# Block products for the whole second layer, worked in quarters, with sums from the float32 values

## The chip, the cores and the metric

The kernel runs on one core of one Trainium2 chip. The metric is the device time of one execution in microseconds, of which the median over the runs is given. The core has five engines that run side by side and wait for one another through semaphores: TensorE (matmul; PE in the profile, PEld for its weight loads), VectorE (DVE), ScalarE (ACT), GpSimd (POOL) and SyncE (SP, which here issues DMAs).

## The reference

An attention with window and block summaries over q, k, v of 2 x 8 x 768 x 64 gives a matrix x of 1536 tokens by 512 features. Two feed-forward layers with 2048 hidden features follow. They take most of the time:

```python
def _moe_ref(x, w_in, w_out):
    h = x @ w_in
    relu6 = np.clip(h + 3.0, 0.0, 6.0)
    g = h * relu6 / 6.0
    return g @ w_out

def _moe2_ref(x, w_in, w_out):
    h = x @ w_in
    g = h * (1.0 / (1.0 + np.exp(-h)))
    return g @ w_out
```

## The kernel before

Every float32 factor is split into a high part that TensorE takes in its one-pass float32 type (fp32r) and the low rest, and a product is made of three matmuls: high x high, high x low, low x high. Weights come from memory as float64, two 32-bit words each, and are turned into float32 by VectorE and ScalarE in the steps `conv_mag`, `conv_low`, `conv_clamp`, `conv_join`, `conv_sign`; `conv_hi` (ScalarE or VectorE) then writes the high part and `conv_lo` (GpSimd or VectorE) the low part into a weight slot. A weight group is 128 hidden features: half h = 2n is its columns of w_in, 2n + 1 its rows of w_out. There are 16 groups per layer, 32 in all, n = 0 to 31.

Tokens are worked in three blocks j = 0, 1, 2 of 512. One step (a line of `STEPS`) is one weight group with one token block: `hidden` makes h in a PSUM bank (12 matmuls of 512 columns, in two parts of six), `act` (ScalarE) and `gate` (VectorE) make g, `gate_hi` and `gate_lo` split it, and `project` adds its second product to four accumulators in four PSUM banks (12 matmuls, in two parts of six). `close` does the same for the last two steps, accumulator by accumulator. When all groups of a chunk are through, `finish` takes the accumulators out: the first chunk of a token block is copied to SBUF by ScalarE, a later one is added there by VectorE (`fold` for one in between, `finish` for the last, which also stores it or, in the first layer, makes x of the second: `finish` casts the high part, `finish_lo` makes the low part).

The first layer and the first half of the second (8 groups) go in halves of 8 groups per token block. In the second half of the second layer token block 2 goes first, in the plain way, and blocks 0 and 1 follow in two quarters of four groups. There the first product of two token blocks with two weight groups, a 2 x 2 block product over halves of the features, is made by seven block products instead of eight (Strassen-Winograd): `tsum` (lines 879 to 891) makes four sums of token parts and `ssum` (903 to 919) four sums of weight parts for each pair p of groups, from the high and low parts that lie in the slots; `t_hi`, `t_lo`, `s_hi` and `s_lo` split them; `prod` (931 to 950) is one block product of six matmuls of 512 columns; `keep` and the joins `u2`, `vee`, `u4`, `c22`, `c21`, `c12`, `c11` add the products up on VectorE; the four results go on as steps of `PAIR` through `act`, `gate`, `gate_hi`, `gate_lo` and `project`.

The order of all work is the list `ORDER`, written out in the file (1893 entries before, 1985 after). Each engine takes its operations in the order of that list; an asterisk puts a copy, cast or subtraction on VectorE instead of ScalarE or GpSimd. Buffers are rings that are handed out in the same order: 12 weight slots (`ws`), 3 buffers of words as fetched, 2 of bits, 1 of magnitudes, 3 of gates (`gs`), 8 PSUM banks. `grow` adds buffers when earlier data is gone; in the kernel before, the buffers of the conversion are given to the sums and to the products' results when the last weight is converted. SyncE issues the weight fetches (`fetch`) and the stores.

Of the kernel before, what the change touches and what calls it, by code (L numbers as in the profile page):

```python
# [20 lines left out]
P = 128  # L21
# [9 lines left out]
KD = DM // P  # L31
# [16 lines left out]
def shape_constants():  # L48
# [34 lines left out]

def chunk_of(i):
    layer, half, o, _, f = STEPS[i]
    j = o // WIDE
    if layer == half == 1 and j < 2:
        return layer, half, j, f // QUARTER
    return layer, half, j
# [4 lines left out]
FIRST = {  # L94
# [9 lines left out]
for p in range(HALF // 2):  # L104
    i = next(n for n, s in enumerate(STEPS) if s == (1, 1, 0, WIDE, 2 * p))
    for n, name in ((i, "k"), (i + 1, "v"), (i + QUARTER, "u"), (i + QUARTER + 1, "d")):
        PAIR[n] = (name, p)

# [78 lines left out]
mixed_hi 23, normal 22*, turn 22, turned 22, conv_join 19, conv_mag 20, project 14 0, project 14 1, project 13  # L187
0, project 13 1, fetch 23, mixed_lo 23, conv_clamp 20, conv_low 20, fetch 22, conv_sign 20, conv_join 20,
load_v 22, mix 22, act 15, gate 15, gate_hi 15*, conv_hi 19*, gate_lo 15, project 15 0, project 15 1, conv_hi
20*, conv_lo 20, mixed_hi 22*, mixed_lo 22, grow 3, mixed_hi 20, fetch 21, mixed_lo 20, hidden 17 0, conv_lo  # L190
19*, conv_low 22, conv_low 21, conv_sign 21, hidden 16 0, hidden 16 1, conv_mag 21, conv_clamp 21, conv_join
21, conv_hi 21*, conv_mag 22, conv_clamp 22, conv_sign 22, conv_join 22, conv_hi 22*, conv_lo 22*, conv_lo
21*, grow 4, conv_mag 23, conv_clamp 23, finish 0 0 1 0, conv_low 23, fetch 24, finish 0 0 1 3, conv_sign 23,
conv_join 23, hidden 20 0, finish 0 0 1 2, hidden 17 1, act 17, gate 17, gate_hi 17*, conv_hi 23*, hidden 21
0, hidden 21 1, fetch 30, hidden 20 1, hidden 18 0, act 16, gate 16, gate_hi 16, gate_lo 16, project 16 0,
project 16 1, act 20, gate 20, conv_lo 23, conv_mag 24, conv_clamp 24, conv_low 24, hidden 22 0, conv_sign 24,
conv_join 24, conv_hi 24*, conv_lo 24*, gate_lo 17, act 21, gate 21, hidden 22 1, gate_hi 21*, gate_lo 21,
fetch 26, conv_low 26, hidden 18 1, act 18, gate 18, fetch 25, conv_low 25, gate_hi 20, conv_sign 25, conv_mag
25, project 21 0, project 21 1, hidden 19 0, hidden 19 1, act 22, project 17 0, conv_clamp 25, conv_join 25,
conv_sign 26, gate 22, project 17 1, conv_mag 26, conv_clamp 26, conv_join 26, conv_hi 25, conv_lo 25*,  # L200
gate_hi 22, gate_lo 22, project 22 0, fetch 27, conv_low 27, gate_hi 18*, gate_lo 18, conv_sign 27, conv_hi
26, project 18 0, project 18 1, conv_mag 27, conv_clamp 27, project 22 1, hidden 24 0, conv_join 27, conv_hi
27, conv_lo 27, act 19, gate 19, gate_hi 19, hidden 26 0, conv_lo 26*, hidden 26 1, fetch 28, conv_low 28,
gate_lo 20, project 20 0, conv_mag 28, conv_clamp 28, gate_lo 19, fetch 29, project 19 0, conv_sign 28,
conv_low 29, conv_join 28, conv_hi 28*, act 26, conv_lo 28*, conv_sign 29, conv_mag 29, conv_clamp 29,
conv_join 29, conv_hi 29*, conv_lo 29*, conv_mag 30, conv_clamp 30, hidden 24 1, act 24, conv_low 30,
conv_sign 30, hidden 23 0, hidden 23 1, conv_join 30, gate 26, project 20 1, conv_hi 30, fetch 33, fetch 31,
conv_lo 30*, hidden 29 0, hidden 29 1, conv_mag 31, act 23, gate 23, conv_low 31, conv_sign 31, gate_hi 23,
gate_lo 23, gate_hi 26, gate_lo 26, project 23 0, fetch 35, conv_clamp 31, conv_join 31, conv_hi 31*, conv_lo
31*, fetch 32, conv_mag 32, project 19 1, project 23 1, conv_low 32, conv_clamp 32, conv_sign 32, finish 0 0 2  # L210
3, conv_join 32, conv_hi 32*, gate 24, gate_hi 24*, conv_lo 32, conv_low 33, hidden 30 0, conv_mag 33, hidden
30 1, finish 0 0 2 1, act 30, gate 30, finish 0 0 2 0, fetch 34, hidden 28 0, conv_clamp 33, conv_sign 33,
conv_join 33, conv_low 34, finish 0 0 2 2, act 29, gate 29, hidden 28 1, conv_sign 34, fetch 37, conv_mag 34,
conv_clamp 34, gate_lo 24, act 28, gate 28, hidden 27 0, hidden 27 1, hidden 25 0, gate_hi 29, project 24 0,
gate_lo 29, project 29 0, project 24 1, project 29 1, conv_join 34, conv_hi 33*, conv_lo 33, conv_hi 34*,
conv_lo 34, act 27, gate_hi 28, gate_lo 28, hidden 34 0, hidden 34 1, finish 0 0 1 1, project 26 0, conv_mag
35, conv_clamp 35, conv_low 35, conv_sign 35, conv_join 35, gate_hi 30*, act 34, project 26 1, fetch 36,
conv_low 36, hidden 35 0, conv_hi 35*, gate 27, hidden 31 0, hidden 31 1, conv_mag 36, conv_clamp 36, gate_lo
30, hidden 25 1, conv_sign 36, conv_join 36, gate_hi 27*, gate_lo 27, gate 34, project 27 0, project 27 1, act
31, act 25, gate 25, gate_hi 25, conv_lo 35, conv_low 37, project 30 0, project 30 1, fetch 38, hidden 32 0,  # L220
hidden 32 1, gate_lo 25, project 25 0, gate 31, project 25 1, act 32, gate_hi 31, gate_lo 31, project 28 0,
project 31 0, hidden 36 0, finish 0 1 0 1, finish 0 1 0 0, gate 32, gate_hi 32, hidden 37 0, conv_hi 36,
hidden 37 1, hidden 33 0, project 28 1, project 31 1, conv_sign 37, gate_lo 32, project 32 0, finish 0 1 0 3,
finish 0 1 0 2, act 37, conv_mag 37, conv_clamp 37, gate 37, gate_hi 37*, gate_lo 37, conv_lo 36*, hidden 35
1, act 35, hidden 33 1, hidden 39 0, act 33, gate 33, gate_hi 33*, gate_lo 33, fetch 41, project 32 1, project
37 0, project 37 1, conv_low 38, conv_join 37, conv_hi 37*, conv_lo 37*, conv_mag 38, conv_sign 38, hidden 36
1, act 36, gate 36, finish_lo 0 2, hidden 39 1, hidden 40 0, hidden 40 1, gate_hi 36, gate_lo 36, fetch 39,
conv_low 39, project 33 0, project 33 1, act 39, gate 35, gate 39, gate_hi 39*, gate_lo 39, project 36 0,
project 36 1, gate_hi 35*, gate_lo 35, conv_clamp 38, conv_join 38, hidden 38 0, hidden 38 1, project 35 0,
project 35 1, conv_mag 39, hidden 43 0, hidden 43 1, conv_sign 39, conv_clamp 39, conv_join 39, gate_hi 34*,  # L230
gate_lo 34, project 34 0, finish_lo 0 1, project 34 1, conv_hi 38*, conv_lo 38*, act 38, gate 38, fetch 40,
conv_low 40, conv_hi 39, gate_hi 38*, gate_lo 38, conv_mag 40, conv_clamp 40, project 38 0, act 40, act 43,
gate 43, gate 40, project 39 0, gate_hi 40, project 38 1, conv_sign 40, conv_join 40, project 39 1, gate_lo
40, project 40 0, finish 0 1 1 0, conv_lo 39, fetch 45, gate_hi 43, project 40 1, finish_lo 0 0, hidden 41 0,
# [127 lines left out]
def attention_moe_kernel(  # L362
# [765 lines left out]
```

## Time and profile before

| | |
|---|---|
| median of 3 runs | 608.94 us (608.93 to 609.13) |
| the profiled execution | 609.09 us |
| its span, first to last instruction | 607.3 us |
| mean granted TensorE clock | 0.994 |
| TensorE busy | 597.3 us, 3188 matmuls |
| VectorE busy | 459.9 us, 1019 instructions |
| ScalarE busy | 252.3 us |
| GpSimd busy | 70.4 us |

The profile gives one execution. Busy time is the sum of an engine's instructions, overlaps counted once. The chain of waits goes back from the last instruction to what released it at each step. The table by stage gives busy time and instruction counts between two moments.

### The profile page before, as it was taken

The page shows a single profiled execution, that of the slowest core. Times are in us where ns is not written, and L with a number is a line of the kernel's source. Part 1 is how long each engine was busy: PE and PEld are TensorE (multiplying, and loading weights), DVE is VectorE, ACT ScalarE, POOL GpSimd, SP SyncE. Part 2 cuts the span into 40 slices and gives each one's busy share as a digit, 9 for nine tenths or more (in the row PEclk, how much of TensorE's full clock was granted, in tenths as well). Part 3 has the DMA queues.
Part 4 walks back from the last instruction along what each step waited for, and adds up shares of the span by engine and source line. Part 5 has one row for each costly group of instructions (what it writes and reads, how often), then busy time and mean ns, then how long its engine had stood idle before and what let it go on. Part 6 is the DMA issues. An engine that isn't in the chain of part 4 may idle for free.

```text
span 607.3 us, 8702 instructions
## 1 busy us (share of the span) xinstructions
PE 597.3 (98%) x3188; PEld 495.2 (82%) x3188; DVE 459.9 (76%) x1019; ACT 252.3 (42%) x591; POOL 70.4 (12%) x86
## 2 busy tenths in 40 slices
PE   7899999999999999999999999999999999999997
PEld 7778888888888888888888888888888888888786
DVE  4889999586698887537789899624247998888984
ACT  4988877664334344123234453131123333231220
POOL 3483430200000001000001010000001000000000
PEclk9799999999999999999999999999999999999999
DMA  9999965130332342202133333300003000000003
GB/s 250 234 226 258 221 166 122 58 108 15 94 110 98 110 130 76 68 1 69 36 104 105 104 105 114 96 0 1 0 1 104 2 0 1 0 37 17 18 17 122
DMA packets 69051, 51.56 MB, mean 85 GB/s; under 512 B 36368, under 2 KB 63504, under 8 KB 69008
## 3 DMA queue, kind: packets, MB, share of 16 engines
q1 hardware_dynamic: 69008, 51.01, 30.8%
q8 instruction: 25, 0.41, 0.3%
q14 instruction: 18, 0.15, 0.1%
HBM read 47.85 MB, written 3.15 MB: 84 GB/s over the span
## 4 chain that ended last, share of the span: by engine, by line
PE 96%; ACT 2%; DVE 1%; POOL 1%; issue 0%; ACTq 0%
PE bank L721 36%; PE bank L792 22%; PE bank L795 22%; PE bank L950 6%; PE bank L613 3%; PE bank L682 2%; PE bank L670 2%; PE bank L508 1%; PE bank L1046 1%; ACT early_w L642 1%; DVE kmax L522 0%; PE bank L557 0%; PE bank L576 0%; POOL early_units L662 0%; ACT early_w L541 0%
## 5 line engine op out<-in xcount | busy, mean ns | idle before, releaser
L721 PE MATMUL bank<-x,w 128*128 128x512 f32 x768 | 184.9, 391 | 0.0
L721 PEld LDWEIGHTS bank<-x,w 128*128 128x128 f32 x768 | 143.1, 188 | 30.0 <-DVE r L762 0.5
L792 PE MATMUL bank<-g,w 128*128 128x512 f32 x576 | 138.3, 392 | 0.0
L795 PE MATMUL bank<-w,g 128*128 128x512 f32 (+1 forms) x588 | 137.1, 385 | 0.0
L795 PEld LDWEIGHTS bank<-w,g 128*128 128x128 f32 x588 | 108.6, 188 | 23.1 <-DVE g L772 1.0
L792 PEld LDWEIGHTS bank<-g,w 128*128 128x128 f32 x576 | 107.1, 188 | 22.2
L458 POOL TENSOR_TENSOR w<-bits,w 128x512 fp32r<-128x512 f32 x25 | 34.0, 1363 | 349.1 <-ACT w L454 193.5
L772 DVE TENSOR_TENSOR g<-r,g 128x512 fp32r<-128x512 f32 x81 | 55.3, 688 | 24.3 <-ACT g L766 22.1
L418 ACT ACTIVATE mag<-words 128x512 f32<-128x512 f32 x64 | 43.1, 674 | 45.5 <-DVE bits L436 37.2
L750 ACT ACTIVATE r<-bank 128x512 f32<-128x512 f32 x48 | 28.5, 597 | 57.8 <-PE bank L721 49.0
L762 DVE TENSOR_TENSOR r<-bank,r 128x512 f32<-128x512 f32 x28 | 19.1, 687 | 37.6 <-ACT r L752 37.5
L436 DVE SCALAR_TENSOR_TENSOR bits<-mag,bits 128x512 uint32<-128x512 uint32 x64 | 44.3, 693 | 1.6
L721 PE MATMUL bank<-x_late,w 128*128 128x512 f32 x192 | 45.0, 389 | 0.0
L443 DVE SCALAR_TENSOR_TENSOR bits<-words,bits 128x512 uint32<-128x512 uint32 x64 | 44.2, 690 | 1.0
L758 DVE SCALAR_TENSOR_TENSOR r<-r,bank 128x512 f32<-128x512 f32 x48 | 32.5, 682 | 13.9 <-ACT r L750 13.6
L721 PEld LDWEIGHTS bank<-x_late,w 128*128 128x128 f32 x192 | 36.0, 188 | 7.5
L766 ACT CAST g<-r 128x512 fp32r<-128x512 f32 x43 | 26.4, 619 | 30.8 <-PE bank L792 13.7
L752 ACT ACTIVATE r<-bank 128x512 f32<-128x512 f32 x28 | 16.5, 596 | 48.8 <-PE bank L721 46.7
L430 DVE TENSOR_SCALAR mag<-mag 128x512 f32<-128x512 f32 x64 | 30.1, 471 | 4.6 <-ACT mag L418 4.3
L423 DVE TENSOR_SCALAR bits<-words 128x512 uint32<-128x512 uint32 x64 | 28.4, 447 | 1.1 <-DMA words<-in_moe_w_in_dram 0.6
L642 ACT ACTIVATE early_w<-early_w,stat 128x120 f32<-128x120 f32 x72 | 27.5, 385 | 3.8 <-DVE stat L628 3.6
L454 ACT CAST w<-bits 128x512 fp32r<-128x512 f32 x32 | 19.7, 617 | 20.7 <-DVE bits L436 20.7
(160 smaller groups left out, 645.6 us busy)
## 6 DMA issues: line engine op xcount, KB each, us to landing
words<-in_moe_w_in_dram SPq DMA_DIRECT2D x32, 512.0 KB, 3.9
words<-in_moe_w_out_dram SPq DMA_DIRECT2D x32, 512.0 KB, 3.4
early_r<-in_v_dram SPq DMA_DIRECT2D x15, 192.0 KB, 4.4
out_dram<-acc SPq DMA_DIRECT2D x11, 256.0 KB, 2.0
early_w<-in_q_dram SPq DMA_DIRECT2D x10, 256.0 KB, 5.9
stage<-in_k_dram SPq DMA_DIRECT2D x3, 512.0 KB, 5.3
stage<-in_v_dram SPq DMA_DIRECT2D x3, 512.0 KB, 7.3
early_w<-in_v_dram SPq DMA_DIRECT2D x3, 512.0 KB, 5.3
```

The lines of the kernel that those rows point to most:

```text
L418: nc.scalar.activation(out=out, in_=low_high(h)[:, 1].bitcast(F32), func=AF.Abs, scale=EXP_SHIFT)
L430: nc.vector.tensor_scalar(out=mag, in0=mag, scalar1=MAG_MIN, scalar2=MAG_MAX, op0=ALU.max, op1=ALU.min)
L436: nc.vector.scalar_tensor_tensor(out=bits, in0=mags.use(h).bitcast(U32), scalar=3, in1=bits, op0=ALU.logical_shift_left, op1=ALU.bitwise_or,)
L443: nc.vector.scalar_tensor_tensor(out=bits, in0=low_high(h)[:, 1], scalar=0x80000000, in1=bits, op0=ALU.bitwise_and, op1=ALU.bitwise_or,)
L458: eng.tensor_tensor(out=w_half(h, 1), in0=bitss.use(h).bitcast(F32), in1=w_half(h, 0).bitcast(F32), op=ALU.subtract,)
L642: nc.scalar.activation(out=pr[:, hp], in_=pr[:, hp], func=AF.Exp, scale=-1.0, bias=st[:, 0, hp : hp + 1], accum_out=st[:, 1, hp : hp + 1],)
L721: nc.tensor.matmul(ps[:, :n], w[:, a, kk * P : (kk + 1) * P], x[:, o // SUB : (o + n) // SUB, b, kk, :], start=(m == 0), stop=(m == last),)
L758: nc.vector.scalar_tensor_tensor(out=r, in0=r, scalar=6.0, in1=ps, op0=ALU.min, op1=ALU.mult)
L772: eng.tensor_tensor(out=g[:, 1, cols], in0=r[:, cols], in1=g[:, 0, cols].bitcast(F32), op=ALU.subtract)
L792: nc.tensor.matmul(ps[:, o : o + n], lhs, g[:, b, shift : shift + n], **flags)
L795: nc.tensor.matmul(ps[:, : len(cols)], g[:, a, rows], rhs, **flags)
L950: nc.tensor.matmul(ps, lhs, rhs, start=(i == 0), stop=(i == 5))
```

## The change

The whole second layer goes in quarters of four weight groups, each with token blocks 2, 0, 1 in this order, and all eight pairs of its groups use the seven block products for blocks 0 and 1. The accumulators of a quarter are copied out after the first quarter and added after the second and third (`fold`, 24 for 8) and the last. The first layer's second half takes its token blocks in the order 2, 0, 1 too.

The sums are made from the float32 values: `ssum` reads the converted bits before they are split (so these buffers are held longer, `bit_users`, and a third one is laid over the constants once these are done with, `grow 8`), and `tsum` reads the first layer's result in its accumulator buffer; each is one instruction where it was two or three. So the features 0 to 255 of x in token block 1 need no split of their own (`only_in_sums`), and their room holds the split weight sums. The sums and the products' results now need room while weights are still converted: one buffer of words becomes the weight sums (`grow 5`) and one weight slot the token sums (`grow 6`), then results (`grow 7`). The result of a gate in `PAIR` stays in its own buffer and the activation takes a temporary one.

`ORDER` is written anew from the attention's end on (entry 724); before that it is the same. In the new list there are 128 `hidden` for 160, 56 `prod` for 28, 28 more joins, 32 `ssum` for 16, `s_hi` 32 for 16 (11 of them on VectorE, for 8), 32 `s_lo` for 16, 8 `keep` for 4 (two on VectorE), 10 `finish_lo` for 12; of `conv_hi` 25 on VectorE for 32, of `conv_lo` 28 for 39, of `gate_hi` 39 for 43, of `t_hi` one for none.

```diff
+QUARTER = HALF // 2
+BLOCKS = (2, 0, 1)
+STEPS += [(0, 1, j * WIDE, WIDE, f) for j in BLOCKS for f in range(HALF)]
 STEPS += [
-    (layer, half, j * WIDE, WIDE, f)
-    for layer, half in ((0, 1), (1, 0))
-    for j in range(NWIDE)
-    for f in range(HALF)
-]
-
-STEPS += [(1, 1, (NWIDE - 1) * WIDE, WIDE, f) for f in range(HALF)]
-QUARTER = HALF // 2
-STEPS += [
-    (1, 1, j * WIDE, WIDE, q * QUARTER + f)
+    (1, half, j * WIDE, WIDE, q * QUARTER + f)
+    for half in range(2)
     for q in range(2)
-    for j in range(2)
+    for j in BLOCKS
     for f in range(QUARTER)
 ]
...
+for i, s in enumerate(STEPS):
+    if s[0] and s[2] == 0 and s[4] % 2 == 0:
+        for n, name in ((0, "k"), (1, "v"), (QUARTER, "u"), (QUARTER + 1, "d")):
+            PAIR[i + n] = (name, weight_of(i) // 2)
+PAIRED = sorted({p for _, p in PAIR.values()})
...
+    def bit_users(h):
+        n, i = divmod(h, 2)
+        return 2 if i or n // 2 not in PAIRED else 5 - n % 2
...
     def act(i):
-        ps = hidden_of(i, "see")
-        r, cols = room(rs, i, 3)
-        if STEPS[i][0] == 0:
-            nc.scalar.activation(out=r[:, cols], in_=ps[:, : STEPS[i][3]], func=AF.Relu, bias=3.0)
+        kind = dict(func=AF.Sigmoid) if STEPS[i][0] else dict(func=AF.Relu, bias=3.0)
+        if i in PAIR:
+            r, ps = rs.take(("temp", i), 1), rs.see(PAIR[i])
         else:
-            nc.scalar.activation(out=r[:, cols], in_=ps, func=AF.Sigmoid)
+            (r, cols), ps = room(rs, i, 2), banks.use(("h", i))[:, : STEPS[i][3]]
+            r = r[:, cols]
+        nc.scalar.activation(out=r, in_=ps, **kind)
...
+    def fold(n, j, m):
+        ps, part, _, _ = gathered((1, n // 2, j, n % 2), m)
+        nc.vector.tensor_tensor(out=part, in0=ps, in1=part, op=ALU.add)
+
+    def only_in_sums(j, m):
+        return j == 1 and m < KD // 2
...
+            if only_in_sums(j, m):
+                return
+            nc.scalar.copy(out=second_x(j)[:, :, 0, m], in_=halves(part))
...
     def tsum(a):
 
-        out = by_feature(whole_t.take(a, 3 if a < 3 else 2))
-        q = {(k, j, b): quarter(k, j, b) for k in range(2) for j in range(2) for b in range(2)}
+        out = whole_t.take(a, 3 if a < 3 else 2)
         if a % 2 == 0:
-            k, j = (1, 1) if a == 2 else (1, 0)
-            terms = [(q[k, j, 0], None), (by_feature(whole_t.use(a // 2)), ALU.subtract)]
-            add_up(out, terms + [(q[k, j, 1], ALU.add)])
+            x, y = whole_x(1 if a == 2 else 0, 1), whole_t.use(a // 2)
         else:
-            plus, minus = {1: ((0, 1), (0, 0)), 3: ((1, 1), (0, 1))}[a]
-            terms = [(q[*plus, 0], None), (q[*minus, 0], ALU.subtract)]
-            add_up(out, terms + [(q[*plus, 1], ALU.add), (q[*minus, 1], ALU.subtract)])
+            x, y = (whole_x(1, 0), whole_x(0, 0)) if a == 1 else (whole_x(1, 1), whole_x(1, 0))
+        nc.vector.tensor_tensor(out=out, in0=x, in1=y, op=ALU.subtract)
...
-        if k in (1, 3):
-            x, y, op = (a21, a22, ALU.add) if k == 1 else (a11, a21, ALU.subtract)
-            terms = [(x[0], None), (y[0], op), (x[1], ALU.add), (y[1], op)]
+
+        def a(row, col):
+            return bitss.use(2 * (2 * p + row)).bitcast(F32)[:, col * SUB : (col + 1) * SUB]
+
+        if k == 1:
+            x, y, op = bitss.see(4 * p + 2).bitcast(F32)[:, :SUB], a(1, 1), ALU.add
         elif k == 2:
-            terms = [(s[:, 0], None)] + [(x, ALU.subtract) for x in a11]
+            x, y, op = s[:, 0], a(0, 0), ALU.subtract
+        elif k == 3:
+            x, y, op = a(0, 0), a(1, 0), ALU.subtract
         else:
-            terms = [(a12[0], None), (s[:, 1], ALU.subtract), (a12[1], ALU.add)]
-        add_up(s[:, k - 1], terms)
+            x, y, op = a(0, 1), s[:, 1], ALU.subtract
+        nc.vector.tensor_tensor(out=s[:, k - 1], in0=x, in1=y, op=op)
...
         elif n == 5:
...
+            t = words.take("gone", 1)
+            whole_s.free.append(t.bitcast(F32).rearrange("p (k n) -> p k n", k=4))
         elif n == 6:
+            i = slot_number[id(ws.take("gone", 1))]
+            values.append(main.tile([P, 2, 2 * DM], F32, tag=f"w{i}", name="sums"))
+            whole_t.free += [values[0][:, b] for b in range(2)]
+        elif n == 7:
             assert not whole_t.held
-            rs.free += [t[:, o : o + DM] for t in whole_t.free for o in (0, DM)]
+            rs.free += [values[0][:, b, o : o + DM] for b in range(2) for o in (0, DM)]
+        elif n == 8:
+            bitss.free.append(cst[:, :DM].bitcast(U32))
```

## Rows read from the trace of the kernel before

**Rows 1.** The page, busy time, share of the span and instructions of each engine.
```profile
PE 597.3 (98%) x3188; PEld 495.2 (82%) x3188; DVE 459.9 (76%) x1019; ACT 252.3 (42%) x591; POOL 70.4 (12%) x86
```
**Rows 2.** Stages: us, busy us (instructions) per engine, granted clock, DMA share, GB/s.
```profile
core 0: us, PE busy (x) PEld busy (x) DVE busy (x) ACT busy (x) POOL busy (x), PEclk, DMA share, GB/s
...
173.00:339.00 166.00, 166.00 (x734) 137.41 (x733) 126.98 (x228) 57.98 (x100) 12.05 (x9) 1.00 0.27 83
339.00:445.00 106.00, 105.97 (x468) 87.42 (x467) 61.89 (x110) 30.30 (x51) 3.95 (x3) 1.00 0.18 55
445.00:604.20 159.20, 159.11 (x710) 131.09 (x709) 131.55 (x233) 46.93 (x82) 3.88 (x3) 1.00 0.08 27
```
**Rows 3.** The chain that ended last: start us, us, engine, line, instructions.
```profile
445.44 5.44 PE bank L721 x24
...
476.76 1.36 PE bank L950 x6
...
584.91 19.24 PE bank L795 x96
```
**Rows 4.** Waits of TensorE's weight loads, 173 to 604 us: total us, times, longest.
```profile
PEld bank L795 <- DVE g L772: 1.0, 3, 0.4
PEld bank L721 <- DVE r L762: 0.5, 1, 0.5
PEld bank L795 <- DVE g L766: 0.2, 1, 0.2
```
**Rows 5.** Instructions by line and form: busy us, mean ns, idle before them.
```profile
L830 DVE TENSOR_TENSOR acc<-bank,acc 128x512 f32<-128x512 f32 x8 | 5.3, 684 | 2.1 <-PE bank L795 2.1
L959 DVE TENSOR_TENSOR r<-bank,r 128x512 f32<-128x512 f32 x5 | 3.4, 683 | 0.0
L927 DVE TENSOR_TENSOR x<-words,x 128x256 fp32r<-128x256 f32 x16 | 6.5, 418 | 0.1
L923 ACT CAST x<-words 128x256 fp32r<-128x256 f32 x8 | 3.1, 402 | 8.1 <-DVE words L877 8.1
L877 DVE TENSOR_TENSOR words<-words,w 128x256 f32<-128x256 f32 x28 | 11.9, 425 | 0.9
L877 DVE TENSOR_TENSOR words<-words,x 128x1024 f32<-128x1024 f32 x6 | 7.4, 1225 | 0.2
L454 ACT CAST w<-bits 128x512 fp32r<-128x512 f32 x32 | 19.7, 617 | 20.7 <-DVE bits L436 20.7
L454 DVE CAST w<-bits 128x512 fp32r<-128x512 f32 x32 | 13.5, 424 | 0.8
L458 DVE TENSOR_TENSOR w<-bits,w 128x512 fp32r<-128x512 f32 x39 | 26.6, 688 | 0.9
L458 POOL TENSOR_TENSOR w<-bits,w 128x512 fp32r<-128x512 f32 x25 | 34.0, 1363 | 349.1 <-ACT w L454 193.5 <-DVE w L454 135.0 <-PE bank L792 20.5
```
**Rows 6.** VectorE in order of time: start us, duration us, line, operation.
```profile
475.00 0.41 DVE L423 TENSOR_SCALAR bits<-words 128x512 uint32<-128x512 uint32 x1
475.33 0.42 DVE L430 TENSOR_SCALAR mag<-mag 128x512 f32<-128x512 f32 x1
475.67 0.68 DVE L443 SCALAR_TENSOR_TENSOR bits<-words,bits 128x512 uint32<-128x512 uint32 x1
476.38 0.69 DVE L436 SCALAR_TENSOR_TENSOR bits<-mag,bits 128x512 uint32<-128x512 uint32 x1
...
577.13 0.68 DVE L762 TENSOR_TENSOR r<-words,r 128x512 f32<-128x512 f32 x1
577.73 0.68 DVE L959 TENSOR_TENSOR bits<-bank,bits 128x512 f32<-128x512 f32 x1
```
**Rows 7.** Stages of VectorE's dense stretch, columns as in rows 2.
```profile
469.60:491.40 21.80, 21.80 (x98) 18.06 (x97) 21.10 (x34) 8.16 (x14) 0.33 (x1) 1.00 0.03 13
491.40:513.20 21.80, 21.80 (x98) 18.06 (x97) 18.33 (x31) 9.09 (x16) 0.00 (x0) 1.00 0.00 1
513.20:534.90 21.70, 21.70 (x98) 17.96 (x97) 18.68 (x34) 4.46 (x8) 0.00 (x0) 1.00 0.03 13
534.90:556.70 21.80, 21.77 (x96) 17.71 (x95) 18.71 (x38) 6.40 (x12) 0.00 (x0) 1.00 0.06 24
556.70:578.40 21.70, 21.70 (x95) 17.49 (x94) 19.21 (x40) 4.49 (x8) 0.00 (x0) 1.00 0.04 14
```

More of the change, by code (lines that the diff above doesn't have):

```diff
@@ L286 @@
-gate_lo 71, conv_mag 63, conv_clamp 63, prod 1 1, keep 1, gate_lo 72, project 69 0, project 71 0, prod 0 1,
-conv_low 63, conv_sign 63, conv_join 63, finish 1 0 2 0, conv_hi 62*, conv_lo 62*, conv_hi 63, conv_lo 63*,
-grow 5, finish 1 0 2 1, hidden 76 0, project 69 1, hidden 73 0, hidden 73 1, tsum 3, hidden 74 1, hidden 76 1,
-hidden 75 0, tsum 1, hidden 75 1, project 71 1, t_hi 3, ssum 0 1, ssum 0 2, s_hi 0 2*, ssum 0 4, finish 1 0 1
-1, act 73, gate 73, s_hi 0 1*, s_lo 0 1, gate_hi 73, act 75, gate 75, gate_hi 75*, finish 1 0 2 3, t_lo 3,
@@ new lines @@
+ssum 9 3, hidden 48 1, gate 44, gate_hi 44*, gate_lo 44, project 44 0, project 44 1, fetch 40, conv_low 40,
+conv_clamp 39, conv_join 39, conv_hi 39, gate_lo 42, gate 47, act 48, gate_hi 47, gate_lo 47, conv_lo 39, gate
+48, gate_hi 48, conv_mag 40, conv_clamp 40, gate_lo 48, project 42 0, project 47 0, finish 0 1 1 1, fetch 41,
+finish 0 1 1 0, tsum 1, project 42 1, project 47 1, finish 0 1 1 2, conv_low 41, prod 8 1, t_hi 1*, finish 0 1
+1 3, hidden 49 0, t_lo 1, keep 8, finish_lo 1 2, tsum 2, tsum 4, t_hi 2, t_lo 2, t_hi 4, t_lo 4, hidden 49 1,
@@ new lines @@
+project 48 0, tsum 3, prod 9 2, hidden 50 0, ssum 9 2, ssum 9 4, prod 8 2, t_hi 3, conv_sign 40, hidden 51 0,
+hidden 51 1, act 49, gate 49, gate_hi 49, prod 8 6, conv_join 40, conv_hi 40, gate_lo 49, t_lo 3, finish_lo 1
+3, conv_lo 40*, hidden 50 1, act 50, gate 50, gate_hi 50, grow 7, project 49 0, act 51, prod 8 7, conv_mag 41,
+u2 8, vee 8, gate 51, conv_clamp 41, prod 8 3, conv_sign 41, c11 8, act 52, conv_join 41, conv_hi 41, gate 52,
+prod 8 5, u4 8, gate_lo 50, s_hi 9 2, s_lo 9 2, project 48 1, prod 8 4, c22 8, c21 8, project 49 1, gate_hi
@@ new lines @@
+1, ssum 12 2, gate_hi 64*, conv_hi 49*, conv_lo 49, project 62 1, project 63 0, ssum 12 3, fold 1 2 0, project
+63 1, prod 11 6, gate 65, fold 1 2 2, prod 11 7, keep 11, gate_hi 65, conv_hi 50, u2 11, fetch 52, ssum 12 4,
+fetch 51, conv_lo 50*, gate_lo 64, prod 11 5, gate_lo 65, prod 11 3, conv_low 52, vee 11, c22 11, u4 11,
+conv_sign 52, act 71, gate 71, prod 11 4, prod 11 2, project 64 0, conv_low 51, c11 11, conv_sign 51, conv_mag
+51, conv_clamp 51, conv_join 51, s_hi 12 2, s_hi 12 4, s_lo 12 4, c21 11, fetch 53, fold 1 2 3, s_hi 12 3*,
@@ new lines @@
+81*, project 73 0, project 73 1, conv_sign 57, conv_join 57, act 77, gate_hi 74, gate_lo 74, prod 13 6, s_hi
+13 4, conv_mag 58, conv_sign 58, gate_hi 75, project 74 0, project 74 1, gate 77, gate_lo 75, conv_hi 57*,
+s_lo 13 4, conv_lo 57*, project 75 0, fold 2 2 0, project 75 1, conv_clamp 58, act 76, gate 76, gate_hi 76,
+fold 2 2 3, prod 13 1, prod 13 7, s_hi 13 1*, gate_lo 76, conv_lo 56, keep 13, u2 13, fold 2 2 1, c11 13,
+gate_lo 81, hidden 84 0, hidden 84 1, s_lo 13 1, prod 13 5, conv_join 58, ssum 14 1, ssum 14 2, prod 13 3, act
@@ new lines @@
+conv_low 60, prod 14 4, fold 2 0 3, gate_hi 83*, prod 14 1, conv_sign 60, fold 2 0 1, conv_mag 60, conv_clamp
+60, project 80 0, project 81 0, gate 82, fold 2 0 2, ssum 14 4, s_hi 14 4, conv_join 60, conv_hi 60, project
+80 1, s_hi 14 3*, s_lo 14 3, project 81 1, gate_hi 82, hidden 85 0, keep 14*, gate_lo 82, project 82 0,
+project 82 1, conv_mag 61, conv_clamp 61, conv_low 61, conv_sign 61, conv_join 61, gate_lo 83, project 83 0,
+fetch 62, conv_mag 62, conv_clamp 62, project 83 1, fold 2 1 1, fetch 63, fold 2 0 0, conv_lo 60, conv_hi 61,
```

334 lines of the change are left out of this document (155 added, 179 removed).

## The prediction

> **What bounds the kernel now.** I read the page first, then the stages, then the chain of waits, then TensorE's own waits, and last VectorE in its dense stretch. The page puts TensorE at 98% of the span and VectorE at 76% [rows 1]. A busy TensorE need not be at its peak, so the next view decides: from 173 us on TensorE is never out of work. From 339 to 445 us it ran 468 matmuls in 106.0 us, 0.2265 us each, at granted clock 1.00, its higher level [rows 2]. The chain says the same per group: 24 matmuls of 512 columns take 5.44 us and a Strassen-type block product of six takes 1.36 us, so 0.2267 us each whatever the line, and the last 96 before the end stand in one piece [rows 3]. All that its weight loads waited for between 173 and 604 us is 1.0 + 0.5 + 0.2 = 1.7 us, each time for VectorE's gate parts [rows 4]. So a matmul taken away is worth 0.2267 us, as long as VectorE, which feeds it, keeps up.
>
> **The part that gains.** In the second layer the first product of token blocks 0 and 1 with two weight groups takes 2 x 2 x 12 = 48 matmuls in the plain way and 7 x 6 = 42 by block products. The kernel has this for the four pairs of the second half; the change has it for all eight. In the order list 32 `hidden` halves of six go and 28 `prod` of six come: 24 matmuls less, 24 x 0.2267 = 5.44 us. `project` and `close` stay as many, and the quarters change only their order.
>
> **What VectorE and the others get.** Durations of single instructions are not what they cost one behind the other. A 128x512 operation with two inputs is 0.68 to 0.69 us long [rows 5], but the next one starts 0.60 us after it (577.13 to 577.73); one with a single input starts its successor after 0.33 us (475.00, 475.33). Only when the successor reads what was just written is it 0.71 us (475.67 to 476.38) [rows 6]. The shorter ones shrink in proportion, 0.42 to 0.34 us for 256 columns (an estimate from the 0.42 and 0.33 of row 475.00), 1.22 to 1.13 for 1024 (the same 0.09 off). At these steps:
> More: 16 `fold` (24 for 8), as the first half's quarters are added too: 9.6 us. Seven joins for each of four pairs, 28: 16.8. 16 `s_lo`: 5.4. Three more `s_hi`, two `keep` and a `t_hi` here: about 2.6. Together 34.4.
> Less: `ssum` from 40 instructions of 256 columns to 32, mostly dependent ones at 0.45: 3.6. `tsum` from ten of 1024 columns to four: 7.3. 11 `conv_lo` that go to GpSimd: 6.6. Seven `conv_hi` and four `gate_hi` that go to ScalarE: 3.7. Two `finish_lo` dropped: 1.2. Together 22.4.
> Net VectorE +12 us, 460 to some 472 of 604: 78%. By full durations it is +15.
> ScalarE gets 13 `s_hi` at 0.40, seven `conv_hi`, four `gate_hi`, two `keep` and loses two casts and one `t_hi`: about +11 on 252 us. GpSimd gets 11 x 1.36 = 15 on 70 [rows 5]. Neither is near its limit. DMA: the same 64 weight fetches and 13 stores on SP's queue; they are spread over the whole second layer, since one word buffer and one weight slot are given up earlier. I cost them at nothing: what hides them is the slack of the buffers, and if that is gone a fetch, four conversion steps and two casts stand in a row ahead of a `hidden`. The tightest slot reuse that I find in the new list (weight group 27) still has five groups of six matmuls, 6.8 us, over the two steps that must wait for the slot, 0.62 on ScalarE and 1.36 on GpSimd. `s_hi` now waits for nothing of token block 1's first features, as these are only needed in sums; what waits at the layer's start is the chain `tsum`, `t_hi`, `t_lo`, with nine groups (12.2 us) between the first layer's last `project` and the first product that needs it; VectorE's work ahead of that is nine instructions, some 8 us by the same steps.
>
> **Where the load is dense.** More than the total, the share per pair matters. In the new steady state a pair of weight groups costs TensorE 7 products, 2 plain firsts of two halves and 6 seconds of two halves: 23 x 1.36 = 31.3 us. VectorE's share of it, when all four weight parts are converted in that time: 33 two-input instructions (7 joins, 6 gates, 6 `gate_lo`, 4.5 folds and finishes, 8 in conversions, 1.75 `conv_lo`) x 0.60 = 20.0; 12 one-input ones x 0.34 = 4.1; 8 of 256 columns and 1.4 casts, 3.1. That is 27.2 us; some 20 of the steps are dependent and add 0.11 each: 29.4, or 94%. By full durations it is 32.2, or 103%. The row nearest to it is the kernel's own product stretch: from 491.4 to 578.4 us VectorE was busy 18.33 + 18.68 + 18.71 + 19.21 = 74.9 of 87.0 us (86%), and in the 21.8 us before that 21.10 (97%), and TensorE waited for next to nothing [rows 4, 7]. So a short load of 97% is known to be harmless and 86% for long; 94% over several pairs lies between. Only about 24 of the 32 second-layer weight parts are converted that late, so six pairs or so are heavy and the rest lighter. I take 29.4, since the steps of rows 6 were taken in just such a stretch.
>
> Here a page speaks against the change. The steps of rows 6 are shorter than the durations. The Trainium skill, "VectorE: DVE Perf Modes", section "The DRAIN you can't avoid", has it that the next operation cannot issue until the pipeline of the last one has emptied; by it the sum of full durations would count, and the gain would be used up. The trace does not agree for independent operations (0.60 after 0.68).
>
> **The sum.** 608.94 - 5.44 = 603.5. For the places where a gate part comes late I add 0.2, as in the trace's 1.7 us over 431 us they are few: 603.7 us. The profiled execution was 609.09 with a span of 607.3, 0.15 above the median and 1.8 outside the span; I keep both offsets, so the span should be about 602.1. The unknown part is what a fuller VectorE costs TensorE: at best nothing, and half of the 1.7 us of late gates goes too, 603.5 - 0.8 = 602.7; at worst the cases below.
>
> **Rivals.**
> VectorE nearly full. It is busy 94%, and its order is fixed, so a join that waits for its product holds back the gates behind it. Of 4.3 us that it would idle per pair at the 14% of rows 7, only 1.9 are free (31.3 - 29.4); if it keeps 2.3 to 2.6, TensorE loses 0.4 to 0.7 in each of six heavy pairs, 2.4 to 4.2 in all: about 606. For it: the 97% stretch is only 21.8 us long. Against: no wait above 0.5 us in a stretch of 86%.
> Full lengths. If each VectorE step costs its full duration under this mix, a heavy pair is 0.9 us over, six of them 5.4: the gain is just given back, 609. This is what the page's rule would do. Against it: rows 6.
> VectorE becomes the bound (slower). Work 29.4 and waits for products, three quarters of the present 4.3 kept, give 32.6 per heavy pair, 1.3 over TensorE's 31.3; six pairs lose 7.8, less 5.4: 611.3. It decides from 32.2 per pair on (31.3 + 5.44 / 6), that is when 2.8 us of waits cannot be given up. For it: 24 folds instead of 8 must free PSUM banks on the engine that is late. Against: a waiting VectorE has other work listed, and in the product stretch of now its waits cost TensorE nothing.
> The change does not do what it says: the products come but something else of six matmuls stays. The list of operations speaks against it (192 matmuls go, 168 come); time as before.
>
> **Chances.** Forecast 0.62; nearly full 0.18; full lengths or no effect 0.09; VectorE as bound 0.11. Differences under 0.2%, 1.2 us, can't be told from none. So faster 0.80, same 0.09, slower 0.11. The range 602.7 to 608.0 leaves out the last two cases, 0.20.
>
> **What would show it.** Right: 3164 matmuls for 3188; the span near 602; the chain one piece of TensorE from 173 us to the end; weight loads' waits still about 2 us; VectorE about 470 us, never above 97% of a stretch. Wrong: waits of weight loads on gate parts, joins or weight conversions of 3 us and more (nearly full), VectorE at 98% or more over 60 us with TensorE idle beside it (VectorE as bound), or steps of 0.69 us between independent operations (full lengths). A lower granted clock in the second layer would make all of this wrong, as it would show that TensorE idled.

## The result and the profile after

The changed kernel takes 602.77 us in the median (602.37 to 602.98, 4 runs) for 609.04 (608.93 to 609.30) of the kernel before beside it: ratio 0.9896, 95% interval 0.9878 to 0.9913. The gain is 6.27 us; 603.7 was forecast, with a range of 602.7 to 608.0. The profiled execution took 602.95 us with a span of 601.1. In the experiments below one run of one kernel (1452.86 us, *Shorter products*) lies far off the others and is left out of its median.

The page of the changed kernel, its first part:

```profile
PE 590.1 (98%) x3164; PEld 489.4 (81%) x3164; DVE 476.4 (79%) x1047; ACT 261.3 (43%) x614; POOL 86.1 (14%) x97
```

24 matmuls are gone [rows 1] and VectorE is busy for 16.5 us more. The stages of the changed kernel, columns as in [rows 2]:

```profile
0.00:47.89 47.89, 41.24 (x436) 36.09 (x437) 38.37 (x157) 36.15 (x122) 28.87 (x44) 0.96 1.09 244
47.89:172.35 124.46, 123.67 (x848) 101.71 (x847) 102.74 (x294) 80.74 (x238) 20.83 (x27) 1.00 0.49 124
172.35:597.98 425.63, 425.21 (x1884) 351.58 (x1883) 334.90 (x597) 144.44 (x256) 36.41 (x26) 1.00 0.18 56
```

And the kernel before, cut at the same three places of the work (first `hidden`, the attention's end, last matmul):

```profile
0.00:49.55 49.55, 42.73 (x436) 37.57 (x437) 37.87 (x157) 36.56 (x122) 29.56 (x44) 0.93 1.05 238
49.55:173.04 123.49, 123.49 (x848) 101.79 (x847) 101.27 (x294) 80.51 (x237) 20.96 (x27) 1.00 0.49 124
173.04:604.15 431.11, 431.04 (x1909) 355.89 (x1907) 320.36 (x569) 135.21 (x233) 19.87 (x15) 1.00 0.18 55
```

The third line of each is the one that the change touches: 431.11 - 425.63 = 5.48 us, which is 24 x 0.2267 = 5.44 within what such a cut can tell (a matmul record or two are missing). The other 0.69 us of the profiled pair comes from before the first changed operation, where the instructions are the same: 1.66 us less in the first stage and 0.97 more in the second. In the first stage the mean granted clock is 0.93 in the kernel before and 0.96 in the changed one, since TensorE ran at its lower level (half clock) for 6.8 us in the one and for 3.4 us in the other.

The weight loads' waits after 172 us, to be held against [rows 4]:

```profile
PEld bank L809 <- DVE g L786: 1.3, 2, 0.7
```

So TensorE hardly waits. VectorE, though, is dense for much longer than before. The same 200 us of the second layer, first in the kernel before, then in the changed one, which has block products all through it:

```profile
345.00:545.00 200.00, 199.94 (x881) 164.81 (x880) 140.70 (x245) 63.05 (x110) 7.83 (x6) 1.00 0.12 37
345.00:545.00 200.00, 199.58 (x879) 164.57 (x878) 180.05 (x325) 75.45 (x136) 21.06 (x15) 1.00 0.19 58
```

180.05 of 200 us is 90%. The chain that ended last shows it too. Its shares of the span by engine, before and after, and the changed kernel's fullest stage:

```profile
PE 96%; ACT 2%; DVE 1%; POOL 1%; issue 0%; ACTq 0%
PE 86%; DVE 7%; ACT 4%; DMA 1%; issue 1%; SPq 0%; DVEq 0%; ACTq 0%
447.90:469.60 21.70, 21.42 (x95) 17.37 (x93) 21.27 (x38) 10.15 (x19) 3.03 (x2) 1.00 0.23 72
```

From 436 to 470 us the changed kernel's chain runs over VectorE, which is busy 98% (21.27 of 21.70 us) in the middle of it, and the two late gates stand at its end (468.3 and 470.1 us). By time and waits alone one would say that a tenth of VectorE is still free. The experiments say what that tenth is worth.

### The profile page after: what moved, and what is told of

The parts are those of the page before. It is cut to its first block, busy times and chain, and to the rows that moved or that the text cites. A ratio compares the mean times of both kernels' runs of the same rounds, so it can differ in the third digit from the quotient of the medians.

```text
span 601.1 us, 8713 instructions
## 1 busy us (share of the span) xinstructions
PE 590.1 (98%) x3164; PEld 489.4 (81%) x3164; DVE 476.4 (79%) x1047; ACT 261.3 (43%) x614; POOL 86.1 (14%) x97
## 4 chain that ended last, share of the span: by engine, by line
PE 86%; DVE 7%; ACT 4%; DMA 1%; issue 1%; SPq 0%; DVEq 0%; ACTq 0%
PE bank L730 27%; PE bank L806 22%; PE bank L809 19%; PE bank L966 11%; PE bank L622 2%; PE bank L691 2%; PE bank L679 1%; PE bank L517 1%; DMA early_w<-in_k_dram 1%; DVE g L786 1%; PE bank L1063 1%; ACT early_units L651 1%; ACT early_w L651 1%; DVE kmax L531 1%; DVE early_w L637 1%
## 5 line engine op out<-in xcount | busy, mean ns | idle before, releaser
L730 PE MATMUL bank<-x,w 128*128 128x512 f32 x576 | 139.8, 392 | 0.0
L730 PEld LDWEIGHTS bank<-x,w 128*128 128x128 f32 x576 | 107.2, 188 | 22.0 <-DVE x L714 0.2
L786 DVE TENSOR_TENSOR g<-r,g 128x512 fp32r<-128x512 f32 x72 | 52.9, 739 | 16.9 <-ACT g L780 15.5
L759 ACT ACTIVATE r<-bank 128x512 f32<-128x512 f32 x60 | 35.4, 596 | 67.2 <-PE bank L730 50.6
L966 PE MATMUL bank<-w,x 128*128 128x512 f32 x144 | 35.7, 389 | 0.0
L452 DVE SCALAR_TENSOR_TENSOR bits<-words,bits 128x512 uint32<-128x512 uint32 x48 | 34.8, 725 | 0.7
L445 DVE SCALAR_TENSOR_TENSOR bits<-mag,bits 128x512 uint32<-128x512 uint32 x48 | 33.1, 689 | 1.0
L966 PEld LDWEIGHTS bank<-w,x 128*128 128x128 f32 x144 | 27.0, 188 | 5.6
L467 POOL TENSOR_TENSOR w<-cst,w 128x512 fp32r<-128x512 f32 x10 | 14.3, 1425 | 88.2 <-ACT w L463 44.0
L432 DVE TENSOR_SCALAR bits<-words 128x512 uint32<-128x512 uint32 x48 | 22.0, 460 | 3.5 <-DMA words<-in_moe_w_in_dram 1.8
```

The costliest lines, as they stand in the source:

```text
L445: nc.vector.scalar_tensor_tensor(out=bits, in0=mags.use(h).bitcast(U32), scalar=3, in1=bits, op0=ALU.logical_shift_left, op1=ALU.bitwise_or,)
L452: nc.vector.scalar_tensor_tensor(out=bits, in0=low_high(h)[:, 1], scalar=0x80000000, in1=bits, op0=ALU.bitwise_and, op1=ALU.bitwise_or,)
L467: eng.tensor_tensor(out=w_half(h, 1), in0=bitss.use(h).bitcast(F32), in1=w_half(h, 0).bitcast(F32), op=ALU.subtract,)
L730: nc.tensor.matmul(ps[:, :n], w[:, a, kk * P : (kk + 1) * P], x[:, o // SUB : (o + n) // SUB, b, kk, :], start=(m == 0), stop=(m == last),)
L759: nc.scalar.activation(out=r, in_=ps, **kind)
L786: eng.tensor_tensor(out=g[:, 1, cols], in0=r[:, cols], in1=g[:, 0, cols].bitcast(F32), op=ALU.subtract)
```

## The experiments

Times of runs beside different runs of the kernel before are compared by their ratios; the changed kernel's is 0.9896, and 0.990 when it was run again. Where a text speaks of the traced stretch, it is the time in the run's trace from the first matmul behind the attention to the end of the last matmul: 431.26 us before, 425.80 in the changed kernel. The start of a run has no part in it.

**The changed kernel again**, for the start.

> The changed kernel itself, unchanged, beside more runs of the kernel before on one chip. Theory 1 (the change is worth 24 matmuls, 5.4 us; the rest of the 6.2 us came from runs of before that all had 6.8 us of half clock at the start): runs of the two kernels with the same mean granted clock differ by 4.9 to 5.6 us, and the medians by 4.9 to 6.5, as the starts fall. Theory 2 (the change shortens the start too): by 6.0 to 6.5 also at the same granted clock.

Median 603.00 us for 608.98 of before (17 runs): ratio 0.990 (0.988 to 0.992). By granted clock the runs fall into groups. Where the mean clock of the run was 0.996 to 1.0, before took 607.25 to 607.79 and this kernel 602.15 and 601.71: 5.1 to 6.1 apart. Where it was 0.993 or 0.994, before took 608.31 to 610.41 with a median of 609.3 (12 runs), and this kernel 603.00 to 603.67: some 6.2. Theory 1's 5.4 lies inside the first of these only, Theory 2's 6.0 to 6.5 holds the second and touches the first, so the times lean to Theory 2. The traces decide against it. The traced stretch of this run is 425.80 us once more, 5.46 less than before: that is what the change is worth. The moment at which the stretch begins differs between traces of the very same instructions: from 172.18 to 172.88 us in the seven traces with 6.8 us at half clock (before has the latest, `b_less24`, which does the same work up to there, the earliest) and from 171.13 to 172.19 in the five with 3.4 or none. The 0.69 us lie within that. A lower clock at the start costs more than that: between the medians of the two groups of runs, 1.7 us for the kernel before and 1.1 for this one, so two kernels' medians of four runs can differ by as much through it alone. In the first comparison before had 0.994 in its profiled run and this kernel 0.994 to 0.997.

**24 matmuls back.**

```diff
+        again = mms if k == 1 and p < 12 else []
-        for i, (kk, (a, b)) in enumerate(mms):
+        for i, (kk, (a, b)) in enumerate(again + mms):
+            i %= 6
```

> The changed kernel, with 24 matmuls added back: the six matmuls of the first block product of pairs 8 to 11 are issued twice, the second time from the start again, so the result is the same. VectorE's work stays. Theory 1: 602.8 + 5.4 = 608.2. Theory 2 (VectorE sets the pace in the dense stretch): some of the added TensorE time fits into its waits, 603 to 606.5.

607.63 us (607.25 to 609.86, 12 runs), ratio 0.9994 (0.9982 to 1.0006). That is 0.0098 x 609 = 6.0 us above the changed kernel; between runs at a clock of 0.997, 607.5 against 602.15 of the run again (one run, on another chip, on which the kernel before takes the same 607.4 at that clock), 5.4; in the traced stretch, 431.16 for 425.80, 5.36. None of the added time fits into a wait. TensorE paces the changed kernel; Theory 2's 603 to 606.5 falls.

**24 matmuls less, in the kernel before.**

```diff
+        if (layer, half, j) == (1, 0, 0) and f % 2 == 0:
+            if part:
+                return
+            last = cut - 1
```

> The kernel before, with 24 matmuls left out: in the first half of the second layer the second six matmuls of the first product of token block 0 with weight groups 16, 18, 20 and 22 are not issued, so these four hold only two of four feature parts. VectorE's work is as before. Theory 1 (TensorE is the bound, each matmul is worth 0.2267 us, and the changed kernel hides all of VectorE's additional work): 608.9 - 5.4 = 603.5, and 24 matmuls explain 5.4 us of the 6.2 us that the change gained; the other 0.7 us lies in the first 50 us of the run and comes from how long TensorE ran at half clock there, so it shows here only if this run's start does. Theory 2 (VectorE's additional work costs the changed kernel something): this kernel, without that work, is the faster one of the two, below 602.4.

604.74 us (604.03 to 605.91, 6 runs) for 608.51: ratio 0.9945 (0.9928 to 0.9963), a gain of 3.3 to 3.8 and not of 5.4; in the traced stretch, 427.93 for 431.26, it is 3.33. This is slower than either theory had it (603.5, or below 602.4). The waits of its weight loads after 173 us:

```profile
PEld bank L799 <- DVE g L776: 2.6, 5, 1.1
PEld bank L799 <- DVE g L770: 0.8, 2, 0.5
PEld bank L725 <- DVE r L766: 0.6, 1, 0.6
PEld bank L799 <- ACT g L770: 0.4, 1, 0.4
```

4.4 us, for 1.7 [rows 4]. The 2.7 us more stand between 344 and 389 us, in and behind the stretch where the matmuls were left out, and most of them cost time (5.44 - 3.33 = 2.1). TensorE waits there for gate parts, which sit in VectorE's list where the removed matmuls used to give them time. Neither theory had this: here a removed matmul is worth 0.2267 us only if the order is laid out anew, as the change does.

**Both sums at their old length.**

```diff
+            for _ in range(2 if k % 2 == 0 else 3):
+                nc.vector.tensor_tensor(out=s[:, k - 1], in0=x, in1=y, op=op)
```

and the same for `tsum`.

> The changed kernel with the token and weight sums at the instruction counts of the kernel before (ten per pair of weight groups, ten for the tokens), by issuing the one instruction two or three times; the values are the same. VectorE gets 48 instructions of 256 columns at 0.34 and 6 of 1024 at 1.13: 16.3 + 6.8 = 23 us. Theory 1 in its strong form (VectorE has room for it): 602.8. Theory 2 (a heavy pair goes from 29.4 to 31.4 us of VectorE work for 31.3 of TensorE): TensorE waits, 604 to 609, and the sums from the float32 values are what lets the block products gain at all.

628.74 us (627.69 to 628.94), ratio 1.0334 (1.0314 to 1.0354): some 26 us above the changed kernel for 23 us of VectorE work by the steps. Theory 2 had the sign and at most a quarter of the size. In the trace TensorE ran at half clock for 10.2 us of the second layer, which is a part of the loss. The next two take it apart.

**Only the token sums long.**

> The changed kernel with only the token sums at the instruction count of before: ten instructions of 1024 columns instead of four, the same values. VectorE gets 6 x 1.13 = 6.8 us, all of it at the start of the second layer in the chain that the first products wait for; the prediction counted 12.2 us of TensorE work over 8 us of VectorE work there. Theory 1: 6.8 less the 4.2 us of room, so 2.6 us: 605.4. Theory 2 (in the run with both sums long, TensorE lost some 9.5 us between 345 and 385 us and its clock fell there): 609 to 613.

610.43 us (608.93 to 612.04, 10 runs) for 608.98, ratio 1.0028 (1.0015 to 1.0041): 7.4 us above the changed kernel run beside it (6.8 in the traced stretch), for 6.8 us of work. The stage at the second layer's start, in the changed kernel and here, and the waits in it here:

```profile
345.00:385.00 40.00, 40.00 (x178) 33.14 (x177) 37.83 (x62) 16.26 (x27) 0.00 (x0) 1.00 0.12 37
345.00:385.00 40.00, 34.92 (x147) 28.19 (x146) 38.89 (x55) 13.48 (x22) 0.00 (x0) 0.96 0.09 27
```

```profile
PEld bank L809 <- ACT g L780: 5.5, 1, 5.5
PEld bank L967 <- DVE w L912: 0.3, 1, 0.3
```

TensorE did 147 matmuls where the changed kernel does 178, and waited 5.5 us in one piece behind the lengthened chain; from 0.6 us before the end of that wait its clock was at half for 3.4 us (0.96 in this stage), which adds about 1.4 more (an estimate: half of the rest). There was no room at the layer's start. The prediction had counted the groups of six that lie between first and last of the chain in the list (12.2 us against 8), and the product that needs the sums did wait only 0.3 us (L967). What it did not count is the plain step behind the chain: its activation (L759) stands in ScalarE's list behind the cast of the last sum, its gate (L773) in VectorE's list behind that sum. The gate came at 367.19 us, where the changed kernel has it at 360.48, and TensorE waited for its gate part.

**Only the weight sums long.**

> The changed kernel with only the weight sums at the instruction count of before: ten instructions of 256 columns per pair of weight groups instead of four, the same values. VectorE gets 2.0 to 2.7 us per pair, 16 to 22 in all. If VectorE had the reserve of the prediction, 1.9 us per heavy pair: 603 to 608. If it has none left in the heavy pairs: 617 to 622.

620.84 us (620.55 to 621.13), ratio 1.0199 (1.0181 to 1.0217): 17.8 us above the changed kernel for 16 to 22 us of added work by the steps. The traced stretch grew by 19.2 us (445.04), of which 3.4 are TensorE's half clock (an estimate: half of two times 3.4 us), and VectorE's busy time in it by 22.8 (357.87 for 335.06). So at 90% busy VectorE had next to no reserve that this order could use. The changed kernel's stages from 425 us on, then this run's:

```profile
425.00:465.00 40.00, 40.00 (x178) 33.14 (x177) 37.09 (x73) 16.12 (x31) 2.99 (x3) 1.00 0.25 78
465.00:505.00 40.00, 39.58 (x174) 32.09 (x173) 34.70 (x61) 12.76 (x24) 7.96 (x6) 1.00 0.22 66
425.00:465.00 40.00, 35.98 (x149) 28.36 (x148) 35.35 (x66) 12.01 (x24) 4.22 (x3) 0.96 0.12 40
465.00:505.00 40.00, 36.96 (x150) 28.60 (x149) 36.16 (x63) 11.96 (x21) 5.78 (x4) 0.96 0.21 66
```

```profile
PEld bank L809 <- DVE g L786: 6.1, 5, 3.3
```

Of the 178 matmuls that 40 us hold, TensorE lost 178 - 149 = 29 and 28, 6.6 and 6.3 us, and VectorE is still busy only 88% and 90%. The longest waits of the two stages are for gate parts. The idle tenth does not go away when VectorE is late: in a fixed order it waits for a product, a cast of ScalarE or an accumulator, and TensorE then waits for it in turn. After waits of 3.3 and 2.2 us TensorE's clock fell to half, once in each of the two stages (0.96).

**Less VectorE work.**

```diff
     def conv_clamp(h):
+        if h >= 38:
+            return
```

> The changed kernel without the step that bounds the magnitudes (conv_clamp) for the weight parts from 38 on, that is for the second layer's parts converted late: 26 VectorE instructions at 0.33 us, 8.6 us less on VectorE. Theory 1 (TensorE is the bound as it stands, VectorE only just keeps up): 602.4 to 603.0, at most the 1.3 us of late gates come back. Theory 2 (VectorE already sets the pace in the dense stretch): 597 to 601.

601.24 us (600.8 to 602.74), ratio 0.9889 (0.9871 to 0.9908), between the two theories' ranges and not told apart from the changed kernel by its interval. At a clock of 0.997 its runs took 600.80 to 600.87, 1.3 us less than the one run of the changed kernel with 602.15; the traced stretch is 1.1 us shorter (424.70), and the trace has no wait of a weight load after 172 us left:

```profile
345.00:545.00 200.00, 200.00 (x884) 165.67 (x883) 171.23 (x303) 75.91 (x138) 20.40 (x15) 1.00 0.18 58
```

So 8.6 us less on VectorE are worth the late gates, 1.1 to 1.3 us, and no more: they make TensorE's stream whole, with VectorE at 86%. That is Theory 1's mechanism, though the median lies below its range. (As the guard against extreme weights is left out, this is no version to use.)

**Shorter products.**

```diff
-        mms = [(kk, ab) for kk in range(2) for ab in ((0, 0), (0, 1), (1, 0))]
+        mms = [(kk, ab) for kk in range(2) for ab in ((0, 0), (0, 1))]
```

> The changed kernel with block products of four matmuls instead of six: the third term of each (low part of the weights with high part of the tokens) is left out, 112 matmuls. Theory 1, if TensorE stayed the bound: 602.8 - 25.4 = 577.4. Theory 2 (VectorE's 29.4 us per heavy pair of weight groups is close to TensorE's 31.3): a pair would take TensorE 31.3 - 3.2 = 28.1, less than VectorE needs, so six heavy pairs give 1.9 each and two light ones 3.2: 602.8 - 17.7 = 585, or more if VectorE cannot give up its waits (590).

> The changed kernel with block products of four matmuls again, for its profile: 591 to 593. If VectorE sets the pace, it is busy 95% and more from 385 us on, and TensorE's weight loads wait 10 to 15 us in all, mostly for gate parts and sums; if buffers do, both engines idle together.

591.38 (three runs) and 591.45 us, both at ratio 0.9728 (0.9705 to 0.975): 10 to 11 us gained of the 25.4 that 112 matmuls take. VectorE's row and the largest waits, from the second:

```profile
345.00:545.00 200.00, 192.33 (x820) 151.30 (x819) 188.14 (x339) 77.28 (x139) 22.54 (x16) 1.00 0.18 58
```

```profile
PEld bank L809 <- DVE g L786: 10.1, 15, 1.9
PEld bank L966 <- DVE r L773: 2.0, 3, 1.3
PEld bank L809 <- DVE r L975: 1.9, 3, 0.9
```

VectorE is at 94% here. From 385 us on, for which 95% and more was expected, it is at 93%, and TensorE waits 20.3 us where 10 to 15 were expected, 15 times for gate parts. A kernel with 25 us less for TensorE would, in this order, be VectorE's.

**Shorter products and no bound on the magnitudes.**

> The changed kernel with both cuts: block products without the third term (112 matmuls less) and no bounding step for the weight parts from 38 on. The first cut alone gave 591.9 of the 577.4 that TensorE alone would allow. If VectorE sets the pace there, 8.6 us less of its work shows nearly whole: 583 to 586. If something else holds it (buffers, the order, ScalarE), 590 to 592.

587.31 us (586.62 to 587.54), ratio 0.9653 (0.9634 to 0.9673): 4.1 to 4.6 us of the 8.6. But all its runs had a clock of 0.994, and most of the others' 0.997; at 0.994 it is 587.3 for 592.5, 5.2 us, and in the traced stretch 409.28 for 415.32, 6.0. That lies between the two theories; VectorE's load is a half to two thirds of what holds this kernel, its waits in the fixed order would be the rest, though no run took them apart.

**The late weights' low parts on VectorE.**

```diff
+ON_DVE |= {("conv_lo", h) for h in range(40, 2 * 2 * NF)}
```

> The changed kernel with all low parts of the weights of groups 20 to 31 subtracted on VectorE (14 of these 24 conversions are on GpSimd now). VectorE gets 14 x 0.60 = 8.4 us more. Theory A (VectorE is nearly full in the heavy pairs, so its load counts): TensorE waits 1 to 6 us more, 604 to 609. Theory B (while GpSimd subtracts, VectorE's operation beside it is held until GpSimd is done, 1.0 to 1.1 us longer than alone in 8 places of the trace, so the move to GpSimd has freed nothing): no slower than the changed kernel, 602 to 603.

606.18 us (605.26 to 606.81), ratio 0.9957 (0.9941 to 0.9973): 3.2 us above the changed kernel, in the traced stretch (429.02) too, so Theory A has the time. But Theory B has a part of it. The edit moves 16 subtractions, not the 14 that were expected. VectorE's busy time in the dense stretch hardly rose, though it had 13 instructions more there:

```profile
345.00:545.00 200.00, 198.42 (x876) 163.86 (x875) 181.81 (x338) 74.80 (x135) 0.00 (x0) 1.00 0.18 58
```

```profile
PEld bank L731 <- DVE w L468: 2.5, 1, 2.5
PEld bank L810 <- DVE g L787: 2.2, 2, 2.0
```

1.8 us more busy, not 8 (3.0 in the traced stretch, for 16 at 0.60); and the time was lost in two waits, 2.5 us for a low part itself and 2.0 for a gate, not by load all along. In this order GpSimd is worth having because the low parts there do not queue behind VectorE's other work, less because they take work off it.

**Filling the gaps at the start.**

```diff
-        for _ in range(2):
+        for _ in range(2 if i < 30 else 8):
```

with `warm 30`, `warm 31` and `warm 32` put into the list at the three gaps.

> The changed kernel with 24 more filling matmuls of 128 columns at three places of the first 22 us where TensorE waits (before the transposes of key tile 2, before the scores of units 3 and 1). They fill gaps in which nothing else can run. If the stretches at half clock in the first 40 us come from these gaps, more runs show a granted clock of 0.997 to 1.0 and the median falls by 0.5 to 1.3 us, to 601.7 to 602.5. If not, or if the filling itself is in the way: 603 to 604.

602.23 us (601.64 to 603.6, 6 runs), ratio 0.9905 (0.9885 to 0.9924). All six runs had a clock of 0.999 or 1.0, so the gaps are what lowers it. The median lies in the range expected for that, but the ratio is not better than the changed kernel's 0.9896 and 0.990: at a clock of 1.0 these runs took 602.0 to 602.8, against 601.71 in the one run of the changed kernel that had it, on another chip. So the filling matmuls may cost what the clock gives back; a gain can't be told. It is no version that beats the change.

## Why the prediction was right

**The gain.** Its step "24 x 0.2267 = 5.44" measured 5.48 in the stretch after 172 us. The assumption under it, that the new order keeps TensorE fed, held: waits of 1.3 us for the 1.7 of [rows 4]. `a_plus24` shows it from the other side: the 24 matmuls put back cost 5.36 us in the traced stretch. `b_less24` shows that this was no matter of course: without a new order 3.3 to 3.8 of the 5.4 were left.

**The remaining 0.7 to 0.8 us** was not forecast. It lies in the start, before any changed operation, where traces of the same instructions differ by as much, with the granted clock and apart from it. That the range's lower end of 602.7 just held it is luck, for the reason behind that end was another (half of the late gates' time coming back), and that did not happen: 1.3 us of 1.7 stayed.

**Two signs named for a right forecast did not come.** The chain is not one piece of TensorE, as it runs over VectorE from 436 to 470 us, and VectorE is at 98% in the stage from 447.9 to 469.6 us, not at most at 97%. So the rival "VectorE nearly full" is there in small: it puts the two late gates where they are, and `a_no_clamp` prices it at 1.1 us in the traced stretch, not at 2.4 to 4.2.

**VectorE's sum.** 472 us was said, 476.4 came. The term that was mis-sized is the 6.6 us for 11 `conv_lo` that go to GpSimd. After 172 us the trace has 15 VectorE operations that are longer than their like, by 10.9 us in all, each of them beside a GpSimd subtraction; before there were seven, 4.7 us. The 6.2 us between them ate that term nearly whole, and are more than the excess over 472.

**The load of a pair.** 29.4 of 31.3 us, 94%, was too much for a mean: 90% over the dense 200 us, that is 28.2, with stages from 87% to 95%. "Full lengths" falls: in the changed kernel's dense stretch independent operations of 0.68 us still start 0.60 apart (next fence, 446.51 to 447.11 and 447.11 to 447.71). Of the Trainium skill, "VectorE: DVE Perf Modes", section "The DRAIN you can't avoid", the sentence by which the next operation does not start until the pipeline is empty does not hold here; the remark in the same paragraph that one that is not held starts earlier, which the prediction passed over, does. VectorE of the changed kernel in order of time:

```profile
446.51 0.68 DVE L786 TENSOR_TENSOR g<-sums,g 128x512 fp32r<-128x512 f32 x1
447.11 0.68 DVE L786 TENSOR_TENSOR g<-r,g 128x512 fp32r<-128x512 f32 x1
447.71 0.41 DVE L432 TENSOR_SCALAR bits<-words 128x512 uint32<-128x512 uint32 x1
```

**The rival "VectorE becomes the bound"** got a chance of 0.11 and a point from which it decides, 32.2 us per pair, with 2.8 us of waits that cannot be given up. The mechanism is real and the step that put it so far off was wrong: it treated idle time as a reserve, of which VectorE would give up most. `a_ssum_long` added 2.0 to 2.7 us per pair to some 28.2 and lost nearly all of it, so about 3 us per pair of waits were kept to the last (an estimate: 31.3 - 28.2), and the rival would have decided with the change's own sums at their old length in this order: 620.8 with the weight sums alone. That the sums are made from the float32 values, which the prediction booked as 11 us less work for VectorE, is what lets the block products gain anything in this order; with the old length in the same list the change would have cost 3.3% (`a_sums_long`). What a list laid out for the longer sums would take, no run shows.

## What to carry to other kernels

When one engine is full and a second at 90% in a fixed order, do not count on the second's idle tenth as a reserve: here it was made of waits that move with the work. So price each instruction added to it at its full step, and expect nothing from those taken away beyond the first engine's remaining waits. Work removed from the full engine is sure to be gained whole only if the other engines' order is laid out for the shorter stream (3.3 of 5.4 us without it here). Before half a microsecond at the start of such a run is put down to a change, compare runs of equal granted clock.

## What was not expected of the hardware

A GpSimd subtraction with two inputs in SBUF holds VectorE. The two engines and TensorE's weight loads in the changed kernel, at one of its two late gates:

```profile
464.64 1.32 POOL L467 TENSOR_TENSOR w<-bits,w 128x512 fp32r<-128x512 f32 x1 [20.74 <-PE bank L809]
464.83 1.68 DVE L764 TENSOR_TENSOR sums<-sums,r 128x512 f32<-128x512 f32 x1
465.92 1.75 POOL L467 TENSOR_TENSOR w<-cst,w 128x512 fp32r<-128x512 f32 x1
466.43 1.79 DVE L786 TENSOR_TENSOR g<-r,g 128x512 fp32r<-128x512 f32 x1
...
468.28 0.53 PEld L809 LDWEIGHTS bank<-w,g 128*128 128x128 f32 x3 [0.70 <-DVE g L786]
```

The VectorE operations take 1.68 and 1.79 us instead of 0.69, each ending 0.55 us after the GpSimd operation that was running when it began, and the second is the gate part that TensorE then waits 0.70 us for. GpSimd is held too at times, 1.75 instead of 1.30. The Trainium skill, "GPSIMD Engine Reference", section "Specifications", says that GpSimd shares its SBUF interfaces with VectorE and contends with operations in a two-port mode or with two SBUF inputs; the trace agrees for two SBUF inputs and gives the size: the lengthened operations lost 0.2 to 1.1 us each, 0.7 in the mean, beside subtractions of 1.3 us. Operations with one input in a PSUM bank (joins, folds, plain gates) were not touched: the 17 that ran beside a subtraction after 172 us took 0.68 to 0.69 us. The gate of a block product reads both inputs from SBUF (L764), so the change itself puts more of VectorE's work in GpSimd's way. Some operations with a single input, in SBUF, were lengthened too (0.42 to 1.36 us).

TensorE's clock at the start differs from run to run of the same kernel: 0.993 to 1.0 in the mean, with 0 to 6.8 us at half clock in the traces, and 1.1 to 1.7 us between the medians of runs with a lower and a higher mean clock. In the middle of a run it fell to half only where TensorE had idled, as in the 5.5 us wait of `a_tsum_long`; in the second run of the shorter products, with 20.3 us of waits in pieces of at most 1.9, it did not fall there.
